# Staged attention values in 128-token groups, their copies behind the product, a conversion's sum one unit later

## The chip, the cores and the metric

The kernel runs on one core of a Trainium2 chip. Its engines work side by side, each through its own queue in program order: TensorE (PE in the profile, with its weight loads as PEld), VectorE (DVE), ScalarE (ACT) and GpSimd (POOL). SyncE (SP) issues nearly all transfers from HBM. The metric is the device time of one execution in microseconds (us), lower is better; it is the median of the runs shown.

## The reference, cut to what matters

Three layers follow one another. Only the first is touched by most of the change; the conversion belongs to the last.

```python
# 1. attention, 4 batches, 8 heads, 512 local and 32 global tokens, head width 64
s_ll = where(|i - j| <= 32, scale * q_l @ k_l.T, -1e9);  s_lg = scale * q_l @ k_g.T
out_l = softmax([s_lg, s_ll]) @ [v_g, v_l]               # a local token sees a window and the global tokens
out_g = softmax(scale * q_g @ [k_g, k_l].T) @ [v_g, v_l] # a global token sees all
# 2. soft mixture of experts: logits = x @ phi, softmax over tokens, 8 experts (w1, relu, w2), softmax over slots
# 3. relu(x @ w_in) ** 2 @ w_out
```

The weights w_in and w_out come as 8-byte floats, read here as pairs of 32-bit words. The kernel turns them into 4-byte floats itself; this is called a conversion.

## The kernel before, in words

**The attention stage** takes the local tokens in 16 blocks of 32. A unit is one block of queries with one half of the heads: `("l", s, e)` for local queries of block s, and `("g", s, e)` for the global queries against the blocks s to s+2, at every third block. There are 44 units. The loop at L703 makes one step n for each unit and a few more, and writes out a software pipeline by hand: step n takes the maximum of unit n's scores on DVE (L327, four at a time) and subtracts it on POOL (L340, called the subtraction n); takes the exponential of unit n-1 on ACT (L349); runs the scores of the next two units on PE (L317); transposes unit n-2 (L357) and copies it out of PSUM (L145 or L147); and in every second step n runs the product of weights and values of the units n-4 and n-3 (L370, `av_at`), followed on DVE by its normalization (L385 to L387). The scores of all units pass through one buffer, `s_buf`, so that the maximum of unit n+1 waits for subtraction n.

`todo[(n, pos)]` holds work for step n at position 0 (before the product), 1 (behind the product and the transposes) or 2 (behind position 1); `late[n]` holds what comes last in a step, mostly transfers. The order on each engine is this written order. SP's queue is in order too: q and k blocks (four transfers of 128 KB for 64 tokens), values, w_in pieces for conversions, and pieces of w1 and w2 for the next layer (512 KB each).

**The values.** A product reads its values from `V`, 96 rows of partitions for three blocks (block i in rows 32*(i%3)), and 32 rows for the global ones. Blocks 1 and 2 are loaded straight into `V` by one transfer (L174). The others pass through `v_next` (128 partitions), filled by transfers of 64 tokens of all batches into one half of its partitions (`load_v_next`, L179, 512 KB, seven times, two of them before the loop) and copied to `V` block by block by `place_v` (L182): batches 0 and 1 by POOL (L188), batches 2 and 3 by ACT (L186). Block s+3 takes the place of block s. It may be copied when the last product with block s's queries is done, and the next pair of products needs it. It is emitted at position 0 of the step behind that product, that is behind the subtraction of that step on POOL. Two blocks fill one transfer, and the half that they leave is loaded again at once.

**The conversions in this stage.** Eight pieces of w_in are converted by five parts: `split` and `rest`, then a step later `clamp` and `shift` (L522, L525) at position 0 and `join` at position 2. `join` makes two instructions: a bitwise one on DVE (L535), and a sum on POOL (L537), which therefore stands ahead of the next step's subtraction on POOL. Steps: `CONV` gives the unit of the first part, 4, 9, 13, 18, 22, 27, 31 and 36.

After the attention (to about 178 us of the span) come the experts and then the last layer, where further conversions run. There the parts of a conversion follow each other in the same order before and after the change.

Of the kernel before, what the change touches and what calls it, by code (L numbers as in the profile page):

```python
# [24 lines left out]
def local_global_attention__soft_moe__relu2_kernel(  # L25
# [15 lines left out]
    nc = tc.nc  # L41
# [131 lines left out]
    def load_v(i, n):  # L173
        nc.sync.dma_start(out=V[QB * i:QB * (i + n), :, :, 0:D].rearrange("p b h d -> p (b h) d"),  # L174
                          in_=v_l[:, :, QB * (i - 1):QB * (i - 1 + n), :].rearrange("b h p d -> p (b h) d"))

    def load_v_next(t):
        p = 2 * QB * (t % 2)
        nc.sync.dma_start(out=v_next[p:p + 2 * QB].rearrange("p b h d -> p (b h) d"),  # L179
                          in_=v_l[:, :, 2 * QB * t:2 * QB * (t + 1), :].rearrange("b h p d -> p (b h) d"))  # L180
# [333 lines left out]
    def convert(raw, dst, y, r, rest_on_act, add):  # L514
# [19 lines left out]
        def join():  # L534
            nc.vector.scalar_tensor_tensor(out=dst, in0=hi, scalar=-0x40000000, in1=yi, op0=ALU.bitwise_and,  # L535
                                           op1=ALU.bitwise_or)
            add.tensor_tensor(out=dst, in0=dst, in1=r, op=ALU.add)  # L537

        return [split, clamp, shift, rest, join]
# [55 lines left out]
    with tc.manual_schedule():  # L595
# [53 lines left out]
        for n in range(NC * WRES):  # L649
            split, clamp, shift, rest, join = win_convert(n)  # L650
            u = units[CONV[n]]
            for f, pos, d in ((split, 2, 0), (rest, 2, 0), (clamp, 0, CONV_AT), (shift, 0, CONV_AT), (join, 2, CONV_AT)):
                at(u, pos, f, d=d)
            if n + 1 < NC * WRES:
                after(u, win_load, n + 1, d=CONV_AT)
# [14 lines left out]
        for s in range(NJ - 2):  # L670
            n = av_at(last_of(s)) + 1
            for i, (b0, b1) in enumerate(((0, 2), (2, 4))):
                todo.setdefault((n, 0), []).insert(0, (place_v, (s + 3, b0, b1, i)))
            if s % 2 and s + 5 < NJ:
                late.setdefault(n, []).insert(0, (load_v_next, ((s + 5) // 2,)))
# [21 lines left out]
        load_v(1, 2)  # L697
        load_vg()
        load_v_next(1)
        load_v_next(2)  # L700
# [133 lines left out]
        def put_convert(q, rest_on_act, first=False):  # L834
# [7 lines left out]
            split, clamp, shift, rest, join = convert(raws[q].rearrange("p (n w) -> p n w", w=2).bitcast(I32),  # L842
# [8 lines left out]
            def last():  # L851
                join()
                room["a"].append(raws[q])
                raw_load()
# [341 lines left out]
```

## Time and profile before

| | us |
|---|---|
| three runs, median | 450.16 |
| lowest and highest of them | 447.58, 450.5 |
| the profiled execution, its own time | 451.68 |
| its span, first to last instruction | 449.9 |

Times in the rows below are microseconds from the span's start, of the one profiled execution. A row of a timeline has start, duration, engine, line, operation, what it writes and reads, and in brackets how long the engine sat idle before it and what ended that. A row of waits has who waited, for whom, the total, how often and the longest.

### The profile page before, as it was taken

What the parts mean: (1) busy time and instruction counts of PE and PEld (TensorE: products, weight loads), DVE (VectorE), ACT (ScalarE), POOL (GpSimd) and SP (SyncE); (2) the same over time, 40 slices, a digit from 0 to 9 for tenths busy, and PEclk for the clock granted to TensorE, in tenths of its full rate; (3) what the DMA queues carried; (4) which work ended last, traced back from release to release, by engine and by line L of the source; (5) the groups of instructions that cost most, each with busy time, mean ns of one, the idle gap of its engine ahead of it and who ended that gap; (6) DMA issues with size and microseconds to landing.
All of it is one profiled execution on the core that took longest, in us unless ns stands there. A gap on an engine that the chain in (4) does not pass through costs nothing.

```text
span 449.9 us, 12265 instructions
## 1 busy us (share of the span) xinstructions
PE 391.8 (87%) x4897; PEld 299.7 (67%) x4897; DVE 285.2 (63%) x911; ACT 223.2 (50%) x455; POOL 143.2 (32%) x173
## 2 busy tenths in 40 slices
PE   6847767877876876799999999999999999999996
PEld 6636555666655655435566778787787888888885
DVE  2426767666775686621089999877998544744443
ACT  1416544745865754212166657465665443444442
POOL 5215354354554553111054543233454000000000
PEclk9987979866998999999999999999999999999999
DMA  7998696989996157999993333320000410320003
GB/s 143 184 172 242 148 265 186 214 222 239 239 267 155 50 189 286 361 369 410 405 366 94 102 94 117 118 93 2 0 1 1 114 27 1 72 70 0 2 1 117
DMA packets 71145, 69.02 MB, mean 153 GB/s; under 512 B 56496, under 2 KB 56752, under 8 KB 71088
## 3 DMA queue, kind: packets, MB, share of 16 engines
q1 hardware_dynamic: 68592, 67.19, 52.3%
q10 hardware_dynamic: 2496, 1.05, 0.9%
q8 instruction: 38, 0.62, 0.6%
q14 instruction: 19, 0.16, 0.1%
HBM read 63.77 MB, written 4.46 MB: 152 GB/s over the span
## 4 chain that ended last, share of the span: by engine, by line
PE 51%; DVE 20%; DMA 9%; issue 8%; POOL 6%; ACT 3%; SPq 1%; POOLq 0%; DVEq 0%; ACTq 0%
PE ops L1129 9%; PE ops L1130 9%; PE ops L1131 8%; PE xp L370 4%; PE pp L357 3%; PE hps L905 3%; PE sp L317 3%; DVE al L1085 3%; DVE arena_a L522 3%; DMA arena_q<-in_q_l_dram 3%; POOL arena_r L340 3%; DVE arena_a L535 3%; DVE arena_b L327 2%; DMA arena_b<-in_moe_w_dram 2%; PE tp L231 2%
## 5 line engine op out<-in xcount | busy, mean ns | idle before, releaser
L1129 PE MATMUL ops<-w_hl,ah 128*128 128x512 f32 x271 | 107.1, 395 | 0.0
L1130 PE MATMUL ops<-w_hl,ah 128*128 128x512 f32 x271 | 106.6, 393 | 0.5 <-POOL w_hl L849 0.5
L1131 PE MATMUL ops<-w_hl,al 128*128 128x512 f32 x271 | 105.8, 390 | 0.0
L1078 DVE TENSOR_TENSOR arena_a<-hp,arena_a 128x384 f32<-128x384 f32 x96 | 46.8, 529 | 45.5 <-ACT arena_a L1077 45.4
L1077 ACT ACTIVATE arena_a<-hp 128x384 f32<-128x384 f32 x96 | 40.2, 471 | 62.2 <-PE hp L1074 61.9
L1084 ACT ACTIVATE ah<-arena_a 128x384 fp32r<-128x384 f32 x96 | 44.9, 504 | 27.9 <-DVE arena_a L1078 27.9
L1130 PEld LDWEIGHTS ops<-w_hl,ah 128*128 128x128 f32 x271 | 50.9, 188 | 11.5 <-POOL w_hl L849 2.7
L1131 PEld LDWEIGHTS ops<-w_hl,al 128*128 128x128 f32 x271 | 50.9, 188 | 11.1 <-DVE al L1085 0.2
L1129 PEld LDWEIGHTS ops<-w_hl,ah 128*128 128x128 f32 x271 | 50.9, 188 | 11.0 <-issue 0.8
L1085 DVE TENSOR_TENSOR al<-arena_a,ah 128x384 fp32r<-128x384 f32 x96 | 50.8, 570 | 8.9 <-ACT ah L1084 4.9
L370 PE MATMUL xp<-arena_v,arena_t 128*32 128x65 f32 x1408 | 30.6, 242 | 23.4 <-POOL arena_v L188 18.9
L340 POOL TENSOR_TENSOR arena_r<-arena_b,nm 128x512 f32<-128x512 f32 x32 | 33.7, 1052 | 51.5 <-DVE nm L327 38.7
L370 PEld LDWEIGHTS xp<-arena_v,arena_t 128*32 128x32 f32 x1408 | 25.5, 123 | 32.8 <-POOL arena_v L188 22.1
L537 POOL TENSOR_TENSOR arena_a<-arena_a 128x512 int32<-128x512 int32 x23 | 29.8, 1294 | 53.1 <-DVE arena_a L535 46.2
L317 PE MATMUL sp<-arena_b 64*32 64x128 f32 x1408 | 31.1, 300 | 6.1 <-issue 3.9
L327 DVE CUSTOM_DVE_ANT_0 arena_b<-sp,arena_r 128x128 f32<-128x128 f32 x128 | 29.4, 285 | 10.2 <-POOL arena_r L340 7.6
L147 ACT ACTIVATE arena_t<-pp 128x512 f32<-128x512 f32 x32 | 19.1, 596 | 27.2 <-PE pp L357 27.1
L357 PE MATMUL pp<-ident,arena_r 128*128 128x128 f32 x176 | 32.5, 315 | 0.0
L349 ACT ACTIVATE arena_r<-arena_r 128x512 f32<-128x512 f32 x44 | 27.6, 627 | 9.2 <-POOL arena_r L340 8.9
L317 PEld LDWEIGHTS sp<-arena_b 64*32 64x32 f32 x1408 | 22.5, 115 | 13.0 <-issue 7.5
L147 ACT ACTIVATE arena_b<-tp 128x512 f32<-128x512 f32 (+1 forms) x31 | 17.5, 579 | 27.2 <-PE tp L231 23.6
L357 PEld LDWEIGHTS pp<-ident,arena_r 128*128 128x128 f32 x176 | 21.9, 158 | 6.2 <-issue 4.1
(192 smaller groups left out, 592.3 us busy)
## 6 DMA issues: line engine op xcount, KB each, us to landing
arena_a<-in_moe_w_dram SPq DMA_DIRECT2D x34, 512.0 KB, 7.4
arena_b<-in_moe_w_dram SPq DMA_DIRECT2D x23, 512.0 KB, 7.7
arena_a<-in_moe_w_out_dram SPq DMA_DIRECT2D x16, 512.0 KB, 5.0
arena_b<-in_moe_w_in_dram SPq DMA_DIRECT2D x8, 512.0 KB, 5.5
arena_a<-in_moe_w_in_dram SPq DMA_DIRECT2D x8, 512.0 KB, 3.9
arena_k<-in_k_l_dram SPq DMA_DIRECT2D x30, 128.0 KB, 5.3
arena_q<-in_q_l_dram SPq DMA_DIRECT2D x30, 128.0 KB, 4.2
arena_b<-in_v_l_dram SPq DMA_DIRECT2D x7, 512.0 KB, 8.3
```

What stands on the lines that cost most here:

```text
L317: nc.tensor.matmul(s_t[n + e][32 * b:32 * b + 32, hp], q, keys, start=True, stop=True, tile_position=(64 * e, 32 * b))
L327: nc.vector.tensor_tensor_reduce(out=s_buf[:, j], in0=sp[:, j], in1=mk, scale=-scale, scalar=BIG, op0=ALU.add, op1=ALU.min, accum_out=nm[: ...
L340: nc.gpsimd.tensor_tensor(out=pe, in0=s_buf, in1=nm.unsqueeze(2).to_broadcast([128, 4, 128]), op=ALU.subtract)
L357: nc.tensor.transpose(pp[:, j], pe_buf[n % NPE][:, j], ident)
L370: nc.tensor.matmul(xp[32 * b:32 * b + 32, hp], pt[:, hp, 32 * b:32 * b + 32], V[:, b, 2 * hp + e], start=True, stop=True)
L1077: nc.scalar.activation(out=r[:, :N], in_=hp[:, :N], func=AF.Relu)
L1078: nc.vector.tensor_tensor(out=a[:, :N], in0=hp[:, :N], in1=r[:, :N], op=ALU.mult)
L1084: nc.scalar.activation(out=ah[:, s], in_=a, func=AF.Copy)
L1085: nc.vector.tensor_tensor(out=al[:, s], in0=a, in1=ah[:, s].bitcast(F32), op=ALU.subtract)
L1129: nc.tensor.matmul(op, ah[:, s], w_hi, start=begin, stop=False)
L1130: nc.tensor.matmul(op, ah[:, s], w_lo, start=False, stop=False)
L1131: nc.tensor.matmul(op, al[:, s], w_hi, start=False, stop=end)
```

## The change

Blocks 1 to 4, 5 to 8, 9 to 12 and 13 to 16 of the values are now loaded as groups of 128 tokens into all 128 partitions of `v_next`, by four transfers (one a batch, 256 KB each); blocks 1 and 2 pass through `v_next` too, so that two more copies run on POOL and two more on ACT, at step 2. A group is loaded again when all four of its blocks have been copied, in the steps 8, 18 and 30. A copy is emitted in the step of the last product that reads the block it replaces, at position 1 behind that product (position 2 for the first block of a group). The sum of a conversion becomes a part of its own, `plus`, emitted at position 0 of the step after `join`.

```diff
-    def load_v(i, n):
...
-    def load_v_next(t):
...
+    def load_v(g):
+        for b in range(B):
+            nc.sync.dma_start(out=v_next[:, b], in_=v_l[b, :, 128 * g:128 * (g + 1), :].rearrange("h p d -> p h d"))
...
         def join():
             nc.vector.scalar_tensor_tensor(out=dst, in0=hi, scalar=-0x40000000, in1=yi, op0=ALU.bitwise_and,
                                            op1=ALU.bitwise_or)
+
+        def plus():
             add.tensor_tensor(out=dst, in0=dst, in1=r, op=ALU.add)
...
-            for f, pos, d in ((split, 2, 0), (rest, 2, 0), (clamp, 0, CONV_AT), (shift, 0, CONV_AT), (join, 2, CONV_AT)):
+            for f, pos, d in ((split, 2, 0), (rest, 2, 0), (clamp, 0, CONV_AT), (shift, 0, CONV_AT), (join, 2, CONV_AT),
+                              (plus, 0, CONV_AT + 1)):
...
-        for s in range(NJ - 2):
-            n = av_at(last_of(s)) + 1
+        for s in range(-2, NJ - 2):
+            n = av_at(last_of(s)) if s >= 0 else 2
             for i, (b0, b1) in enumerate(((0, 2), (2, 4))):
-                todo.setdefault((n, 0), []).insert(0, (place_v, (s + 3, b0, b1, i)))
-            if s % 2 and s + 5 < NJ:
-                late.setdefault(n, []).insert(0, (load_v_next, ((s + 5) // 2,)))
+                todo.setdefault((n, 2 if s % 4 == 2 else 1), []).insert(0, (place_v, (s + 3, b0, b1, i)))
+            if s % 4 == 1 and s + 4 < NJ:
+                late.setdefault(n, []).insert(0, (load_v, ((s + 3) // 4,)))
...
-        load_v(1, 2)
+        load_v(0)
         load_vg()
-        load_v_next(1)
-        load_v_next(2)
```

On PE and DVE the order of instructions is the same before and after. It changes on POOL, ACT and SP; three places follow. In the changed kernel the line numbers are 3 to 5 smaller: the subtraction is L335, the copy on POOL L183, the sum L534, the loads of values L175.

The first place is POOL at the start of the attention, subtractions of the steps 0 to 4 (`arena_r<-arena_b`; `nm` is a unit's maximum). Before:

```order
L340 TENSOR_TENSOR arena_r_99<-arena_b_91,nm_267 128x512
L340 TENSOR_TENSOR arena_r_99<-arena_b_91,nm_285 128x512
L340 TENSOR_TENSOR arena_r_99<-arena_b_91 128x512 x2
L340 TENSOR_TENSOR arena_r_99<-arena_b_91,nm_411 128x512
L340 TENSOR_TENSOR arena_r_99<-arena_b_91,nm_473 128x512
```

After:

```order
L335 TENSOR_TENSOR arena_r_99<-arena_b_91,nm_268 128x512
L335 TENSOR_TENSOR arena_r_99<-arena_b_91,nm_286 128x512
L335 TENSOR_TENSOR arena_r_99<-arena_b_91 128x512
L183 COPY arena_v_95<-arena_b_91 32x16x64 x2
L335 TENSOR_TENSOR arena_r_99<-arena_b_91 128x512
L335 TENSOR_TENSOR arena_r_99<-arena_b_91,nm_416 128x512
```

The two copies of the blocks 1 and 2 now stand between the subtractions 2 and 3. They wait for the first load of values.

The second place is POOL a little later, from subtraction 5 on: the first sum of a conversion (`arena_a<-arena_a,arena_b`) and the copy of block 3 (`arena_v<-arena_b`). Before:

```order
L340 TENSOR_TENSOR arena_r_99<-arena_b_91,nm_473 128x512
L537 TENSOR_TENSOR arena_a_75<-arena_a_75,arena_b_91 128x512
L340 TENSOR_TENSOR arena_r_99<-arena_b_91,nm_540 128x512
L340 TENSOR_TENSOR arena_r_99<-arena_b_91,nm_599 128x512
L188 COPY arena_v_95<-arena_b_91 32x16x64
L340 TENSOR_TENSOR arena_r_99<-arena_b_91,nm_654 128x512
```

After:

```order
L335 TENSOR_TENSOR arena_r_99<-arena_b_91,nm_478 128x512
L335 TENSOR_TENSOR arena_r_99<-arena_b_91,nm_544 128x512
L534 TENSOR_TENSOR arena_a_75<-arena_a_75,arena_b_91 128x512
L183 COPY arena_v_95<-arena_b_91 32x16x64
L335 TENSOR_TENSOR arena_r_99<-arena_b_91,nm_606 128x512
L335 TENSOR_TENSOR arena_r_99<-arena_b_91,nm_659 128x512
```

The sum went from ahead of subtraction 6 to behind it, the copy from behind subtraction 7 to ahead of it.

The third place is SP late in the attention, around step 30: four transfers of k, a piece of w_in, a piece of w1, then q and values. Before:

```order
L162 DMA arena_k<-in_k_l_dram 64x8x64 x4
L512 DMA arena_b<-in_moe_w_in_dram 128x1024
L575 DMA arena_b<-in_moe_w_dram 128x1024
L162 DMA arena_q<-in_q_l_dram 64x8x64 x4
L179 DMA arena_b<-in_v_l_dram 64x32x64
```

After:

```order
L162 DMA arena_k<-in_k_l_dram 64x8x64 x4
L507 DMA arena_b<-in_moe_w_in_dram 128x1024
L572 DMA arena_b<-in_moe_w_dram 128x1024
L175 DMA arena_b<-in_v_l_dram 128x8x64 x4
L162 DMA arena_q<-in_q_l_dram 64x8x64 x4
```

A whole group of values, 1 MB instead of 512 KB, now stands ahead of the q load, where the half group stood behind it.

## Rows read from the trace of the kernel before

**Rows 1.** Busy time by stage: stretch, length, engines, PE clock, DMA share, GB/s.

```profile
60.00:108.00 48.00, 36.08 (x914) 29.06 (x918) 30.68 (x149) 26.22 (x48) 23.51 (x23) 0.79 0.89 230
...
178.00:233.00 55.00, 51.50 (x685) 27.30 (x685) 21.45 (x71) 16.63 (x40) 9.43 (x28) 1.00 1.00 391
```

**Rows 2.** Waits of DVE, 12 to 178 us.

```profile
DVE rd L385 <- PE xp L370: 10.7, 10, 1.9
DVE arena_b L327 <- POOL arena_r L340: 9.6, 13, 1.5
```

**Rows 3.** Waits of PE, 12 to 178 us.

```profile
PE xp L370 <- POOL arena_v L188: 18.9, 9, 3.5
```

**Rows 4.** Timeline of POOL, 57 to 67 us.

```profile
60.58 1.03 POOL L188 COPY arena_v<-arena_b 32x1024 f32<-32x1024 f32 x1
61.69 1.04 POOL L340 TENSOR_TENSOR arena_r<-arena_b,nm 128x512 f32<-128x512 f32 x1
```

**Rows 5.** Timeline of DVE, 60.8 to 64 us.

```profile
62.83 0.17 DVE L385 TENSOR_SCALAR rd<-xp 128x4 f32<-128x4 f32 x1 [1.92 <-PE xp L370]
```

**Rows 6.** Timeline of SP, 14.9 to 34 us: issue, duration of the issue.

```profile
14.97 0.66 SPq L174 DMA_DIRECT2D arena_v<-in_v_l_dram  x1
...
18.15 4.63 SPq L179 DMA_DIRECT2D arena_b<-in_v_l_dram  x2
...
28.92 1.79 SPq L512 DMA_DIRECT2D arena_b<-in_moe_w_in_dram  x1
```

**Rows 7.** Timeline of DVE, 33 to 38.5 us.

```profile
34.60 0.43 DVE L532 TENSOR_SCALAR arena_b<-arena_b 128x512 int32<-128x512 uint32 x1 [8.63 <-DMA arena_b<-in_moe_w_in_dram]
```

**Rows 8.** DMA view, 19 to 29 us: GB/s in 40 slices, packets of the stretch.

```profile
GB/s 230 224 178 152 143 138 121 134 142 144 168 161 172 165 162 159 154 150 141 188 164 162 162 175 177 162 157 161 163 161 153 179 147 138 145 119 138 126 182 124
DMA packets 6086, 1.58 MB, mean 158 GB/s; under 512 B 6083, under 2 KB 6083, under 8 KB 6083
```

**Rows 9.** DMA view, 129.9 to 136 us: GB/s in 40 slices.

```profile
GB/s 96 96 232 149 163 215 134 134 188 349 349 349 349 349 376 349 322 376 403 430 430 336 366 322 254 359 269 265 272 267 264 260 262 235 191 155 99 54 24 15
```

**Rows 10.** The page's part 6, q transfers: KB of one, us to landing.

```profile
arena_q<-in_q_l_dram SPq DMA_DIRECT2D x30, 128.0 KB, 4.2
```

**Rows 11.** Timeline of POOL, 73 to 77.5 us.

```profile
73.60 1.27 POOL L537 TENSOR_TENSOR arena_a<-arena_a,arena_b 128x512 int32<-128x512 int32 x1 [2.29 <-DVE arena_a L535]
74.83 1.04 POOL L340 TENSOR_TENSOR arena_r<-arena_b,nm 128x512 f32<-128x512 f32 x1
```

**Rows 12.** Timeline of DVE, 73 to 76 us.

```profile
74.01 0.28 DVE L327 CUSTOM_DVE_ANT_0 arena_b<-sp,arena_r 128x128 f32<-128x128 f32 x1
```

**Rows 13.** Timeline of PE, 129 to 146 us.

```profile
129.99 1.13 PE L370 MATMUL xp<-arena_v,arena_t 128*32 128x65 f32 x64
...
137.88 0.90 PE L231 MATMUL tp<-arena_b,arena_q 128*128 128x128 f32 x4
...
142.50 0.44 PE L317 MATMUL sp<-arena_b 64*32 64x128 f32 x10 [2.72 <-issue]
```

**Rows 14.** Timeline of SP, 127 to 142 us.

```profile
129.98 2.71 SPq L162 DMA_DIRECT2D arena_q<-in_q_l_dram  x4
```

**Rows 15.** PE groups, 61.6 to 67.6 us: busy, mean ns of one, idle before.

```profile
L357 PE MATMUL pp<-ident,arena_r 128*128 128x128 f32 x8 | 2.2, 433 | 0.0
L370 PE MATMUL xp<-arena_v,arena_t 128*32 128x65 f32 x64 | 2.0, 315 | 3.3 <-POOL arena_v L188 3.3
L317 PE MATMUL sp<-arena_b 64*32 64x128 f32 x64 | 2.0, 418 | 0.0
```

**Rows 16.** PE groups, 151.4 to 155.9 us.

```profile
L357 PE MATMUL pp<-ident,arena_r 128*128 128x128 f32 x8 | 1.3, 286 | 0.0
L317 PE MATMUL sp<-arena_b 64*32 64x128 f32 x64 | 1.2, 274 | 0.0
L370 PE MATMUL xp<-arena_v,arena_t 128*32 128x65 f32 x64 | 1.1, 221 | 1.7 <-POOL arena_v L188 1.7
```

**Rows 17.** The instructions of L525, the shift: duration ns min/median/max.

```profile
L525 DVE TENSOR_SCALAR arena_b<-arena_b x8: 426/1144/1149, 36.2 to 157.2; 128x512 int32<-128x512 int32 x8
```

More of the change, by code (lines that the diff above doesn't have):

```diff
@@ L171, in load_k @@
         load_pair(k_buf, k_l, QB * (i - 1), (1, 3) if i == 1 else ())
-    def load_v(i, n):
-        nc.sync.dma_start(out=V[QB * i:QB * (i + n), :, :, 0:D].rearrange("p b h d -> p (b h) d"),
-                          in_=v_l[:, :, QB * (i - 1):QB * (i - 1 + n), :].rearrange("b h p d -> p (b h) d"))
-    def load_v_next(t):
-        p = 2 * QB * (t % 2)
-        nc.sync.dma_start(out=v_next[p:p + 2 * QB].rearrange("p b h d -> p (b h) d"),
-                          in_=v_l[:, :, 2 * QB * t:2 * QB * (t + 1), :].rearrange("b h p d -> p (b h) d"))
+    def load_v(g):
+        for b in range(B):
+            nc.sync.dma_start(out=v_next[:, b], in_=v_l[b, :, 128 * g:128 * (g + 1), :].rearrange("h p d -> p h d"))
     def place_v(i, b0, b1, who):
@@ L536, in join @@
                                            op1=ALU.bitwise_or)
+        def plus():
             add.tensor_tensor(out=dst, in0=dst, in1=r, op=ALU.add)
-        return [split, clamp, shift, rest, join]
+        return [split, clamp, shift, rest, join, plus]
     CW = 512
@@ L649, in local_global_attention__soft_moe__relu2_kernel @@
         for n in range(NC * WRES):
-            split, clamp, shift, rest, join = win_convert(n)
+            split, clamp, shift, rest, join, plus = win_convert(n)
             u = units[CONV[n]]
-            for f, pos, d in ((split, 2, 0), (rest, 2, 0), (clamp, 0, CONV_AT), (shift, 0, CONV_AT), (join, 2, CONV_AT)):
+            for f, pos, d in ((split, 2, 0), (rest, 2, 0), (clamp, 0, CONV_AT), (shift, 0, CONV_AT), (join, 2, CONV_AT),
+                              (plus, 0, CONV_AT + 1)):
                 at(u, pos, f, d=d)
@@ L841, in put_convert @@
                 o = win2[c][:, CW * f:CW * f + CW]
-            split, clamp, shift, rest, join = convert(raws[q].rearrange("p (n w) -> p n w", w=2).bitcast(I32),
+            split, clamp, shift, rest, join, plus = convert(raws[q].rearrange("p (n w) -> p n w", w=2).bitcast(I32),
                                                       o.bitcast(I32), y[:, 0:DM], y[:, DM:].bitcast(I32),
@@ L852, in last @@
                 join()
+                plus()
                 room["a"].append(raws[q])
```

## The prediction, as it was made

> **What bounds the kernel now.** I read the busy time by stage first. From 178 to 233 us the DMA engines are full (share 1.00, 391 GB/s), so the experts' stage is set by when its transfers can start, and that is when the attention gives up its buffers [rows 1]. Behind it PE is nearly always busy in the last layer, where the change moves nothing. So a microsecond saved or lost in the attention stage goes through to the end almost whole, and only that stage has to be worked out. From 60 to 108 us no engine is full in it: PE 36.1 of 48 us at a granted clock of 0.79, DVE 30.7, POOL 23.5, while the DMA share is 0.89 [rows 1]. Such a stage is set by its chain of waits. The waits come second: PE stood still 18.9 us in nine products because the copy of a value block on POOL was not done [rows 3]; DVE waited 10.7 us for products and 9.6 us for POOL's subtraction [rows 2]. One place shows the pattern: the copy runs on POOL from 60.58 to 61.61, product and subtraction start behind it at once [rows 4, 15], and DVE, idle for 1.92 us, normalizes at 62.83 [rows 5]. Third come the transfers: at 34.60 DVE had waited 8.63 us for the first w_in piece [rows 7], issued only at 28.92 behind the values [rows 6].
>
> **The start.** Before: one value load into `V` at 14.97, then two into `v_next` [rows 6], 0.52 MB each. From 19 to 29 us, where the latter two make up most of the traffic, 256-byte packets moved at 158 GB/s [rows 8]. Each of them goes into one half of the partitions. The q load in the middle of the second stretch, with packets of the same size but spread over both halves, shows 260 to 272 GB/s [rows 9]. The new loads span all 128 partitions; I take 265 for them, the nearest row in shape, and keep 158 as the other end. DMA time removed: 2 x 0.52 MB / 158 = 6.6 us and 0.52 / 265 = 2.0 us; added: 1.05 / 265 = 4.0 us. The w_in piece lands 4.6 us earlier, near 30.0. Against it stand the two copies on POOL and the two on ACT (1.03 us each by the row of a copy [rows 4], ACT's taken alike), which now hold both engines at step 2 until the values are there: four issues of 0.66 us [rows 6] end at 17.6, the data at about 24, ACT's copies at 26, and exponential, transposition and first product follow near 27, their normalization near 29.4. That is just ahead of the new 30.0, so the wait for w_in covers the late product; if the cover is gone, it costs up to 5 us. PE's own work behind that product comes some 0.8 us later than the piece allows. I take -3.8; bounds -4.6 and +1.
>
> **The copies.** In the new order a copy waits for the product and stands ahead of the next subtraction instead of behind it, so the next product, two steps later, finds its values in place. Bounds: 0, if other waits take its place, and -18.9, PE's whole wait [rows 3]. What can reach the end is nearer to DVE's wait for products, 10.7 us [rows 2]. I take half, -5.0: DVE's next step still needs the subtraction, for which it already waits 9.6 us, and PE the copies out of PSUM. What is late next is the subtraction, then a q or k transfer. The copy's new wait for its product holds what is queued behind it on POOL, the next subtraction; but product and subtraction start together [rows 4, 15], and before the next subtraction DVE has to normalize and take four maxima, beside which a copy of 1.03 us fits.
>
> **The sum of a conversion.** Eight sums of 1.27 us stand ahead of a subtraction now. At 73.60 the sum runs until 74.87, DVE's maxima are done at 74.29, and the subtraction starts at 74.83 [rows 11, 12]: 0.5 us each at most, 8 x 0.5 = 4.0. Behind the subtraction the sum of 1.27 us stands beside DVE's four maxima, some 1.0 us (four of at most 0.28 [rows 12]), and can hold the next subtraction by 0.3 us: +2.4. I take -1.5, since DVE has other work in those steps more often than not.
>
> **Lighter transfers.** The reloads in the steps 8, 18 and 30 take 4.0 us each where their halves took 6.6. Two lie in the part where the DMA share is 0.89 [rows 1]: 0 to -5.2, I take -1.0, as most of it ends in idle DMA time. SP issues eight transfers more, 8 x 0.66 = 5.3 us; its waits for buffers to become free cover them.
>
> **New waits.** A group is loaded only when its last block is copied, and the next block is copied two steps later (in the steps 10 and 32; at 22 four steps later). At step 30 the product starts at 129.99 [rows 13]; the copies are done near 133.4, the reload's four issues end near 135.7. Only then q is issued, whose four took 2.71 us from 129.98 before [rows 14]: now until 138.4, the last landing 4.2 us [rows 10] behind its own issue at 137.7, at 141.9. PE wants q at 137.88 [rows 13]. Behind it came the scores, which in the trace stopped for 2.72 us of "issue" and ended at 142.94 [rows 13]. After: 141.9 plus transposition [rows 13] and scores [rows 16] (0.9 and 1.2 us) is 144.0, or 145 at the lower clock. I take +1.0; bounds 0 and +3.5, if that stop of 2.72 us stays behind. At step 8 the same sum leaves q just in time and ACT's copies about half a microsecond late: +0.5; bounds 0 and +3.
>
> **Sum.** -3.8 - 5.0 - 1.5 - 1.0 + 1.5 = -9.8. On the profiled execution's own 451.68 us (its span of 449.9 and 1.8 around it) that is 441.9. The median of the runs shown is 1.5 us lower, so I forecast 440.4 us, 2.2% less. From the bounds of the terms that I hold likely its own range is 436.5 to 444.5.
>
> **Rivals.** (A) PE's clock: more is gained. Behind the wait of 3.3 us that ended with the copy of 60.58 PE worked at the lower of its two levels: transposition, scores and product took 2.2, 2.0 and 2.0 us [rows 15], against 1.3, 1.2 and 1.1 us behind a wait of 1.7 us [rows 16], 2.6 us in all. If two such rounds go to the higher level, 5.2 us come on top: 435.2. For it speaks the clock of 0.79 from 60 to 108 us [rows 1]; against it, that part of PE's low clock lies behind waits for transfers. Chance 0.15.
>
> (B) No change that counts: the new loads move at 158 GB/s like the old. Then the start gives -2.8 (only 0.52 MB less), the lighter transfers nothing, step 8 costs +0.5, and at step 30 a load of 6.6 us instead of 4.0 puts q near 144.5 and the scores 3.9 us late. With k and q late, 1.5 us of the copies' gain goes: -2.8 - 3.5 - 1.5 + 0.5 + 3.9 = -3.4, some 447 us. For it speaks that all packets stay at 256 bytes; against it the rate of the q load [rows 9]. The Trainium skill (SBUF — State Buffer, "Door 1: The DMA port swizzle") says that partitions 0 to 63, or 64 to 127, reach half of the ports that a transfer over all 128 reaches; that is on the side of 265, and B would have a higher chance without it. Chance 0.2.
>
> (C) Slower: a whole group of values stands in SP's queue ahead of q, loaded late. If at both tight places (steps 8 and 30) 6.6 us of transfer at 158 GB/s find no cover and PE restarts at its lower level (0.9 us for one product, 2.0 against 1.1 [rows 15, 16]), they cost 2 x 7.5 = 15.0 us. Against -2.8 at the start, -5.0 and -1.5 that leaves +5.7: 455.9. It decides as soon as the two waits together exceed the 9.3 us of those gains. For it speaks the order of SP at step 30; against it the stop of 2.72 us that is there anyway. Chance 0.12.
>
> (D) POOL's copies hold up DVE. The shift of a conversion takes 0.43 us alone, but 1.14 us in the median [rows 17]: it runs beside a subtraction on POOL. In the steps 10, 14 and 32 a copy now follows on POOL in the step of a shift. If it gets in first, the shift waits out its 1.03 us [rows 4]: 3 x 1.03 = 3.1, and the time is 443.5. The Trainium skill (SBUF — State Buffer, "Who interferes with whom") says of DVE and GpSimd that whichever issues first holds a shared port pair for the whole instruction while the other is blocked; the two levels of the shift agree. Against D: the subtraction is first in its step, and the copy waits for its product. Chance 0.1.
>
> **How the numbers follow.** The forecast has 0.43, A 0.15, B 0.2, C 0.12, D 0.1. A measurement of this kernel tells about 1% from no change, 4.5 us: faster below 445.7, slower above 454.7. Faster: the forecast, A, D and a fifth of B, 0.43 + 0.15 + 0.1 + 0.04 = 0.72, less 0.03 for the upper edges of the forecast and D. No change: the rest of B and that, 0.16 + 0.03 = 0.19. Slower: C, 0.12. The range reaches from 433, a little under A, to 452, above B and D, and leaves out most of C.
>
> **What would show it.** Right: PE's products wait for no copy, and DVE's wait for products falls to half; DVE's first wait for w_in ends near 30; the value loads show about 265 GB/s; POOL's subtractions follow DVE's maxima without a sum between. Wrong: ACT or POOL standing at a copy for a value transfer in the steps 10 or 32, PE standing at the q transposition of step 32 for more than 4 us, or the experts' stage starting no earlier than 174 us.

## The result, and the profile after

The changed kernel takes 445.49 us (median of 20 runs, 441.55 to 450.61), the kernel before in the same comparison 450.25 us. The ratio is 0.9894 with a 95% interval of 0.9867 to 0.9921: 4.8 us faster, where 9.8 us were forecast. The direction held, and the time lies in the whole range given (433 to 452) but above the forecast's own (436.5 to 444.5); the size is a little under half of what was forecast. The profiled execution whose rows follow took 448.08 us by its own time, longer than the median.

Busy time by stage after the change, which answers to [rows 1]:

```profile
60.00:108.00 48.00, 35.40 (x956) 27.24 (x960) 34.24 (x172) 27.93 (x51) 25.05 (x26) 0.89 0.85 239
...
178.00:233.00 55.00, 52.46 (x614) 28.00 (x615) 21.49 (x67) 17.34 (x42) 11.88 (x30) 1.00 0.98 380
```

In the middle of the attention DVE and POOL do more in the same 48 us, and PE's granted clock is 0.89 instead of 0.79. The experts' stage is still full of transfers.

The waits of DVE and PE from 12 to 178 us, after the change. They answer to [rows 2, 3]:

```profile
DVE arena_b L322 <- POOL arena_r L335: 12.8, 13, 2.8
...
PE tp L226 <- DMA arena_q<-in_q_l_dram: 12.1, 4, 5.5
...
PE tp L226 <- DMA arena_k<-in_k_l_dram: 7.0, 6, 2.5
PE xp L365 <- DMA arena_v<-in_v_g_dram: 5.6, 1, 5.6
DVE rd L380 <- PE xp L365: 5.5, 5, 2.7
...
PE xp L365 <- POOL arena_v L183: 0.8, 1, 0.8
```

PE's 18.9 us of waits for POOL's copies are down to 0.8, and DVE's waits for products have halved. Two waits of PE are new: 12.1 us for q, at two places that are shown below, and 5.6 us for the first values (the row names the global values, which come last in that load).

The start, which answers to [rows 6, 7]: SP's issues of the first group and of the first w_in piece, ACT's two copies at step 2, and DVE's first use of that piece.

```profile
15.01 4.92 SPq L175 DMA_DIRECT2D arena_b<-in_v_l_dram  x4
...
25.18 0.92 SPq L507 DMA_DIRECT2D arena_b<-in_moe_w_in_dram  x1
```

```profile
25.10 2.12 ACT L181 ACTIVATE arena_v<-arena_b 32x1024 f32<-32x1024 f32 x2 [6.12 <-DMA arena_b<-in_v_l_dram]
```

```profile
30.33 0.42 DVE L527 TENSOR_SCALAR arena_b<-arena_b 128x512 int32<-128x512 uint32 x1
```

This part came as forecast: the copies wait for the values until 25.1, and DVE takes up the w_in piece at 30.33 instead of 34.60, with no wait left in front of it.

How the lead goes on can be followed on ACT. Exponential n stands once in each step, and its start in two timelines tells how far one kernel is ahead of the other. The table gives the start in the kernel before and, for the others, the difference to it, in us; the labels of the experiments are explained below.

| exponential | 5 | 10 | 20 | 31 | 32 | 43 (last) |
|---|---|---|---|---|---|---|
| before, start | 37.13 | 55.03 | 96.78 | 138.27 | 139.74 | 175.15 |
| changed kernel | -2.4 | +0.1 | -6.6 | -6.2 | +0.2 | -4.5 |
| x6, first group alone | -5.6 | -1.3 | -0.9 | -3.1 | -2.7 | -2.6 |
| x9, x6 with k ahead | -3.1 | -4.0 | -2.7 | -4.6 | -4.0 | -4.1 |
| x11, copies alone | -1.0 | +1.4 | -5.8 | -6.8 | -5.0 | -10.1 |
| y1, changed, k ahead | -3.9 | -2.3 | -11.3 | -8.8 | -2.2 | -6.9 |
| y2, changed, last group by halves | -5.3 | -3.7 | -11.6 | -10.7 | -9.5 | -12.5 |
| x10, all, halves, k ahead | -4.4 | -6.1 | -11.3 | -12.0 | -10.8 | -14.2 |

Each line of the table is one execution, so a single number of it says little: y2 and the changed kernel are issued in the same order until about step 24, and yet their leads at exponential 20 are 5.0 us apart. What repeats from one execution to the next is a fall within one step. In the changed kernel the lead goes between the exponentials 5 and 10 (by 2.5 us; the copies alone lose as much there), and all at once between 31 and 32, where 6.5 us go. Here is the second place, on POOL, SP, PE and ACT; it answers to [rows 13, 14]:

```profile
127.14 1.04 POOL L183 COPY arena_v<-arena_b 32x1024 f32<-32x1024 f32 x1 [0.31 <-PE xp L365]
```

```profile
128.21 3.84 SPq L175 DMA_DIRECT2D arena_b<-in_v_l_dram  x4
132.15 3.25 SPq L162 DMA_DIRECT2D arena_q<-in_q_l_dram  x4
```

```profile
125.88 1.13 PE L365 MATMUL xp<-arena_v,arena_t 128*32 128x65 f32 x64
...
127.52 1.16 PE L312 MATMUL sp<-arena_b 64*32 64x128 f32 x64
...
131.16 0.66 PE L352 MATMUL pp<-ident,arena_r 128*128 128x128 f32 x4
137.21 0.45 PE L226 MATMUL tp<-arena_b,arena_q 128*128 128x128 f32 x1 [5.39 <-DMA arena_q<-in_q_l_dram]
138.57 0.87 PE L226 MATMUL tp<-arena_b,arena_q 128*128 128x128 f32 x3 [0.92 <-DMA arena_q<-in_q_l_dram]
139.37 1.96 PE L312 MATMUL sp<-arena_b 64*32 64x128 f32 x64
```

```profile
136.04 1.06 ACT L181 ACTIVATE arena_v<-arena_b 32x1024 f32<-32x1024 f32 x1 [2.92 <-DMA arena_b<-in_v_l_dram]
```

The reload of the group is issued from 128.21 on, when POOL's copy is done. The four issues of q follow at 132.15. PE is ready for q at 131.8 (137.21 less 5.39) and has all of it at 138.57, and the scores behind it take 1.96 us, against the 1.16 us that such scores took at 127.52: the granted clock is 0.50 from 137 to 142 us, the lower of its two levels. ACT stands at the next copy as well. Both are signs that the prediction named as speaking against it.

These 6.3 us are only half of PE's 12.1 us for q. The other half lies between the exponentials 22 and 23, on SP and PE:

```profile
90.26 1.18 SPq L572 DMA_DIRECT2D arena_a<-in_moe_w_dram  x2
91.54 5.05 SPq L162 DMA_DIRECT2D arena_q<-in_q_l_dram  x4
```

```profile
100.76 0.47 PE L226 MATMUL tp<-arena_b,arena_q 128*128 128x128 f32 x1 [5.54 <-DMA arena_q<-in_q_l_dram]
101.52 0.90 PE L226 MATMUL tp<-arena_b,arena_q 128*128 128x128 f32 x3 [0.28 <-DMA arena_q<-in_q_l_dram]
```

This q load stands behind the reload of step 18 (84.08 to 88.00), four pieces of w1 and one of w_in. The group is not needed for the wait: x5 and x10, which load halves, stand there for 6.4 and 4.7 us. The lead falls by 1.9 us from exponential 22 to 23; no run takes this wait away by itself.

### The profile page after: what moved, and what is told of

The parts are those of the page before. It is cut to its first block, busy times and chain, and to the rows that moved or that the text cites. A ratio compares the mean times of both kernels' runs of the same rounds, so it can differ in the third digit from the quotient of the medians.

```text
span 446.3 us, 12296 instructions
## 1 busy us (share of the span) xinstructions
PE 391.1 (88%) x4897; PEld 295.9 (66%) x4897; DVE 285.1 (64%) x911; ACT 224.3 (50%) x457; POOL 144.4 (32%) x175
## 4 chain that ended last, share of the span: by engine, by line
PE 52%; DVE 17%; DMA 13%; ACT 5%; issue 5%; SPq 5%; POOL 2%; ACTq 1%; POOLq 0%; DVEq 0%
PE ops L1126 9%; PE ops L1127 9%; PE ops L1128 9%; PE sp L312 4%; DMA arena_k<-in_k_l_dram 4%; PE pp L352 3%; PE hps L902 3%; PE xp L365 3%; SPq L162 3%; DVE arena_a L517 3%; DVE arena_a L530 2%; DVE al L1082 2%; DMA arena_b<-in_moe_w_dram 2%; PE tp L226 2%; PE hp L1071 2%
## 5 line engine op out<-in xcount | busy, mean ns | idle before, releaser
L335 POOL TENSOR_TENSOR arena_r<-arena_b,nm 128x512 f32<-128x512 f32 x32 | 33.4, 1042 | 55.9 <-DVE nm L322 30.4
L534 POOL TENSOR_TENSOR arena_a<-arena_a 128x512 int32<-128x512 int32 x23 | 29.7, 1292 | 53.1 <-DVE arena_a L530 46.2
L365 PEld LDWEIGHTS xp<-arena_v,arena_t 128*32 128x32 f32 x1408 | 24.3, 116 | 24.0 <-issue 14.9
L312 PE MATMUL sp<-arena_b 64*32 64x128 f32 x1408 | 32.8, 300 | 4.9 <-ACT arena_b L147 1.8
L312 PEld LDWEIGHTS sp<-arena_b 64*32 64x32 f32 x1408 | 23.2, 115 | 12.5 <-issue 4.7
L352 PE MATMUL pp<-ident,arena_r 128*128 128x128 f32 x176 | 30.5, 300 | 0.0
L845 POOL TENSOR_TENSOR w_hl<-arena_a,w_hl 128x512 fp32r<-128x512 f32 x16 | 21.1, 1319 | 15.1 <-ACT w_hl L844 15.1
```

The lines of the kernel that those rows point to most:

```text
L312: nc.tensor.matmul(s_t[n + e][32 * b:32 * b + 32, hp], q, keys, start=True, stop=True, tile_position=(64 * e, 32 * b))
L335: nc.gpsimd.tensor_tensor(out=pe, in0=s_buf, in1=nm.unsqueeze(2).to_broadcast([128, 4, 128]), op=ALU.subtract)
L352: nc.tensor.transpose(pp[:, j], pe_buf[n % NPE][:, j], ident)
L365: nc.tensor.matmul(xp[32 * b:32 * b + 32, hp], pt[:, hp, 32 * b:32 * b + 32], V[:, b, 2 * hp + e], start=True, stop=True)
```

## Experiments

All runs are compared with the kernel before on the same chip; it measured 448.7 to 451.7 us in the comparisons, so ratios of different comparisons stand side by side only to about 0.5%. The runs x1 to x4, x5 to x8, x9 to x12, y1 to y4, and z1 with z2 are one comparison each.

| run | what differs | ratio to before, 95% | median us |
|---|---|---|---|
| x1 | copies and sum, old loads, each reload in the copy's step | 0.9925 (0.9892 to 0.9959) | 446.36 |
| x2 | group loads alone | 1.0042 (1.0008 to 1.0076) | 452.05 |
| x3 | changed kernel, q ahead of the reload | 0.9899 (0.9853 to 0.9946) | 445.66 |
| x4 | changed kernel, reloads by halves in the copy's step | 0.9940 (0.9901 to 0.9978) | 448.68 |
| x5 | changed kernel, reloads by halves one step later | 0.9816 (0.9766 to 0.9866) | 441.95 |
| x6 | first group alone | 1.0005 (0.9972 to 1.0038) | 449.49 |
| x7 | copies and sum, all transfers as before | 0.9841 (0.9799 to 0.9883) | 441.83 |
| x8 | sum alone | 0.9995 (0.9962 to 1.0029) | 448.39 |
| x9 | x6, w1 pieces behind the k load | 0.9819 (0.9776 to 0.9861) | 443.32 |
| x10 | x5, w1 pieces behind the k load | 0.9739 (0.9701 to 0.9776) | 439.51 |
| x11 | copies alone | 0.9756 (0.9716 to 0.9795) | 440.24 |
| x12 | x7, w1 pieces behind the k load | 0.9766 (0.9723 to 0.9808) | 441.37 |
| y1 | changed kernel, w1 pieces behind the k load | 0.9842 (0.9799 to 0.9884) | 442.46 |
| y2 | changed kernel, last group by halves | 0.9778 (0.9737 to 0.9818) | 439.00 |
| y3 | changed kernel, sum in its old place | 0.9879 (0.9840 to 0.9918) | 445.05 |
| y4 | x10, sum in its old place | 0.9728 (0.9684 to 0.9773) | 438.50 |
| z1 | kernel before, w1 pieces behind the k load | 0.9976 (0.9943 to 1.0008) | 448.37 |
| z2 | y1 and y2 together | 0.9774 (0.9734 to 0.9815) | 438.55 |

**The reload ahead of q.** The first theory, T1, was that copies, sum and start bring what was forecast and that the group reloads ahead of q give it back. x1 takes the copies and the sum without the group loads:

```diff
-            n = av_at(last_of(s)) + 1
+            n = av_at(last_of(s))
...
-                todo.setdefault((n, 0), []).insert(0, (place_v, (s + 3, b0, b1, i)))
+                todo.setdefault((n, 2 if s % 4 == 2 else 1), []).insert(0, (place_v, (s + 3, b0, b1, i)))
```

Expected:

> The kernel before with the copies behind the product and the sum one unit later, but with the old transfers (blocks 1 and 2 straight into V, 64 tokens into one half of v_next, reloaded in the step of the second copy). Theory T1 (the copies and the sum bring about what was forecast, and the group reloads in the queue ahead of q give much of it back): -6.5 us, ratio 0.985, which is lower than that of the changed kernel (0.989). Rival R1 (most of the measured gain is the start; copies and sum bring little, as the subtraction takes the place of the copy): -1 us, ratio 0.998. Rival R2 (a copy on POOL holds DVE's shift): as R1, with shifts of over 1.1 us in more than half of the cases.

x2 takes the group loads and leaves copies and sum where they were. Expected:

> The kernel before with the transfers of 128 tokens alone: blocks 1 and 2 pass through v_next at step 2, copies otherwise one step behind the product at position 0 as before, sum as before, a group loaded again in that later step. T1: the start gives -3.8, lighter transfers -1, and q late behind the reloads +5 or more (the reload is one step later still): 0 to +3 us, ratio 1.000 to 1.007. R1: -4 us, ratio 0.991.

x3 inserts `load_v` behind `load_q` in the list of a step. Expected:

> The changed kernel with one edit: in the steps where a group of values is loaded again, the load of q that stands in the same step (blocks 6 and 14 of the queries) is issued ahead of it. T1: PE's wait of 5.4 us for q near 137 us goes, and the time is 3 to 5 us below the changed kernel, ratio to before 0.980; the values of the next copy come 2.7 us later, which costs at most 1. If the wait only goes from q to the copies' values: ratio 0.989 as the changed kernel, with ACT and POOL standing 3 us longer at their copies in steps 10 and 32.

x4 keeps the first group and reloads with `load_v_next`, from step 2 on. Expected:

> The changed kernel with the first load of values over all 128 partitions, but each later load again of 64 tokens into one half, as soon as its two blocks are copied (six loads in the loop, from step 2 on, two steps or more of slack). T1: the start, the copies and the sum bring -3.8 - 5.0 - 1.5, nothing waits anew: 440 us, ratio 0.978. Rival: the loads at 158 GB/s in the part where the transfers fill 85% of the time delay q and k as much as the groups do: ratio 0.989 or more.

The group loads by themselves are slower, so the loads do cost (in x2 each reload stands one step later still than in the changed kernel). But x1 with no group in it misses T1's number, and its timelines of SP and PE show why:

```profile
132.66 0.62 SPq L179 DMA_DIRECT2D arena_b<-in_v_l_dram  x1
133.37 4.80 SPq L162 DMA_DIRECT2D arena_q<-in_q_l_dram  x4
```

```profile
141.01 0.45 PE L231 MATMUL tp<-arena_b,arena_q 128*128 128x128 f32 x1 [5.97 <-DMA arena_q<-in_q_l_dram]
```

The copy's earlier step had taken the reload with it, and a half of 512 KB ahead of q costs PE the same wait. In x3 q is on time, and the wait only moves to the copy, as the timelines of ACT and PE show:

```profile
140.71 1.06 ACT L181 ACTIVATE arena_v<-arena_b 32x1024 f32<-32x1024 f32 x1 [4.72 <-DMA arena_b<-in_v_l_dram]
```

```profile
141.82 0.65 PE L365 MATMUL xp<-arena_v,arena_t 128*32 128x65 f32 x28 [1.71 <-ACT arena_v L181]
```

So it is not the order of q and values that matters, as T1 had it: at this place a whole group is not loaded in time between the copy that frees it and the copy, two steps on, that needs it. x4 could not show this: its later halves stand ahead of q as in x1, and its first one stands ahead of the first w_in piece, on SP:

```profile
27.95 0.62 SPq L179 DMA_DIRECT2D arena_b<-in_v_l_dram  x1
28.61 1.37 SPq L512 DMA_DIRECT2D arena_b<-in_moe_w_in_dram  x1
```

That piece was issued at 25.18 in the changed kernel, so the start's gain was gone at once.

**The parts apart.** The second theory, T2: the reload's short time is the loss, whichever transfer goes first. x7 is x1 with each reload in its old step, one behind the copy:

```diff
-                late.setdefault(n, []).insert(0, (load_v_next, ((s + 5) // 2,)))
+                late.setdefault(n + 1, []).insert(0, (load_v_next, ((s + 5) // 2,)))
```

Expected:

> The kernel before with the copies behind the product and the sum one unit later, all transfers where they were (each reload one step behind its copy, behind q at step 31). T2: the wait of 6 us for q at step 32 that the first of these kernels showed goes, and the copies and the sum bring -6.5 us, ratio 0.9855. R3: no better than with the reload in the step of the copy, ratio 0.9925.

x5 is the changed kernel with such reloads, the first of them at step 4. Expected:

> The changed kernel with the first group of values, the copies and the sum as they are, but the later values loaded again by halves of 64 tokens in the steps of the kernel before (one step behind the copy, behind q where both meet; the half of blocks 5 and 6 at step 4, behind the first piece of w_in). Theory T2 (a group that is loaded again and needed two steps later costs a wait at steps 8 to 10 and 30 to 33, be it of q, as in the changed kernel, or of the copies, as with q issued first; nothing else was mis-sized): -3.8 - 5.0 - 1.5 = -10 us, ratio 0.977 to 0.980, and PE's waits for q and ACT's for values in the steps 8 to 10 and 30 to 33 gone. Rival R3 (the transfers as a whole bind that part: any microsecond won there turns into a wait for q or k): ratio 0.989 or more.

x6 takes only the first group. Expected:

> The kernel before with the first transfers alone changed: blocks 1 to 4 by one group over all partitions, blocks 1 and 2 copied at step 2, the half of blocks 5 and 6 loaded at step 4 behind the first piece of w_in; all later copies, loads and the sum as before. T2: -3.8 us, ratio 0.9915. R3: -1 us or nothing, as the time won at step 4 is gone by step 10.

x8 takes only the sum. Expected:

> The kernel before with the sum of a conversion alone one unit later. Forecast for this term: -1.5 us, ratio 0.9965; bounds -4.0 (0.991) and +2.4 (1.005).

x11 takes only the copies; it was set up after x5 to x8 were known. Expected:

> The kernel before with the copies behind the product alone, all transfers and the sum as before. If the sum is worth nothing in this company too, as it was alone (0.9995): ratio 0.984, as copies and sum together. If the sum brings its forecast 1.5 us only once the copies no longer stand in the way: ratio 0.9875.

T2 held for x7 and nearly for x5, and fell for the start: x6 measures no gain. The sum alone measures nothing, at most 1.7 us by its interval. The copies alone bring 11.0 us of 451.7 in x11 (0.9756). If the sum is worth nothing, x7 measures the same copies, and there they bring 7.1 us of 448.7 (0.9841). The two intervals do not meet, and nothing but the sum and the comparison differs, so the copies are known only as 7 to 11 us; by either they bring more than the 5.0 of the forecast. Waits of DVE and PE in x11, which answer to [rows 2, 3], and its busy time by stage, to [rows 1]:

```profile
DVE arena_b L327 <- POOL arena_r L340: 11.5, 16, 1.5
...
PE tp L231 <- DMA arena_k<-in_k_l_dram: 11.1, 6, 3.7
...
PE xp L370 <- DMA arena_v<-in_v_g_dram: 1.9, 1, 1.9
...
DVE rd L385 <- PE xp L370: 1.2, 3, 0.7
```

```profile
60.00:108.00 48.00, 37.52 (x1045) 29.04 (x1034) 35.55 (x175) 29.04 (x53) 27.01 (x28) 0.93 1.03 263
```

PE waits for no copy, and DVE's wait for products is all but gone, not halved. The wait for the subtraction has grown by 1.9 us only. In x7 the same two rows are 2.0 and 12.0 us. The clock from 60 to 108 us is 0.93 in x11 and 0.96 in x7.

**What takes back the start.** In the table x6 is 5.6 us ahead at exponential 5 and 1.3 at 10. SP and PE of x6 between them:

```profile
34.60 0.91 SPq L575 DMA_DIRECT2D arena_a<-in_moe_w_dram  x2
35.61 4.20 SPq L162 DMA_DIRECT2D arena_k<-in_k_l_dram  x4
```

```profile
43.71 0.45 PE L231 MATMUL tp<-arena_b,arena_k 128*128 128x128 f32 x1 [2.40 <-DMA arena_k<-in_k_l_dram]
44.83 0.87 PE L231 MATMUL tp<-arena_b,arena_k 128*128 128x128 f32 x3 [0.67 <-DMA arena_k<-in_k_l_dram]
45.49 1.06 PE L231 MATMUL tp<-arena_b,arena_q 128*128 128x128 f32 x4
46.48 1.93 PE L317 MATMUL sp<-arena_b 64*32 64x128 f32 x60
```

The k load stands behind two pieces of w1, 1 MB together; PE waits for it and goes on at the lower clock (0.50 from 43.6 to 48.5 us). Theory T3 is that this takes the start back. The edit moves the pieces from step 5 to step 7 in the table that places them:

```diff
-        0, 0, 0, 0, 1, 2, 0, 0, 1, 1, 1, 1, 0, 1, 1, 1, 0, 0, 2, 2, 1, 0, 1, 1, 0, 1, 2, 1, 0, 1, 0, 0,
+        0, 0, 0, 0, 1, 0, 0, 2, 1, 1, 1, 1, 0, 1, 1, 1, 0, 0, 2, 2, 1, 0, 1, 1, 0, 1, 2, 1, 0, 1, 0, 0,
```

x9, on x6. Expected:

> The kernel with the first group of values alone changed, and one edit more: the two pieces of w1 (512 KB each) that stand in the queue at step 5, ahead of the load of k of step 6, are issued at step 7 behind it. Theory T3 (the start does bring some 5 us until step 7, and the k load behind those pieces, whose landing PE awaits at step 8, takes most of it back): PE's wait for k near 44 us goes and 2 to 3 us come through to the end, ratio 0.994. Rival R3 (the transfers bind the whole stretch to 108 us, so the wait only moves to the next q or k): ratio 1.000 as without the edit.

x10, on x5. Expected:

> The kernel with the first group, the copies and the sum changed and the later values loaded by halves, with the two pieces of w1 of step 5 issued at step 7 behind the k load. T3: PE's wait of 5.9 us for k at step 8 goes, -3 us against the same kernel without the edit (0.9816): ratio 0.975. R3: 0.981 as without it.

x12, on x7. Expected:

> The kernel before with the copies behind the product and the sum one unit later, all value transfers as before, and the two pieces of w1 of step 5 issued at step 7 behind the k load. Without the earlier start the k load is less late there: T3 expects -1 to -2 us against the same kernel without the edit (0.9841): ratio 0.981, and the kernel with the first group on top (the run before the last) 2 us or more lower. R3: 0.984.

z1, on the kernel before. Expected:

> The kernel before with the two pieces of w1 of step 5 issued at step 7 behind the k load, and nothing else. If the k load holds up only what the earlier start has won (T3): -1 us or nothing, ratio 0.998 to 1.000, and the start is worth the difference to 0.982. If the pieces cost the kernel before as much: ratio 0.985 or less, and the start is worth 1 us or less.

In x9 the k load goes ahead of the pieces, and PE transposes it with no wait in front:

```profile
36.45 3.60 SPq L162 DMA_DIRECT2D arena_k<-in_k_l_dram  x4
40.10 1.09 SPq L575 DMA_DIRECT2D arena_a<-in_moe_w_dram  x2
```

```profile
43.91 0.81 PE L231 MATMUL tp<-arena_b,arena_k 128*128 128x128 f32 x4
44.56 0.60 PE L231 MATMUL tp<-arena_b,arena_q 128*128 128x128 f32 x4
```

The time falls to 0.9819, further than T3's 0.994, while the same edit in the kernel before (z1) brings about 1 us, 0.9976. So the start alone does bring time, once k is not late: some 7 us by the two ratios. How much is not settled, as the two traces show less: x9 is 4.1 us ahead at the last exponential, and z1, the edit without the start, is 2.0 us ahead there too. In x10 the edit brings 2.4 us on x5 by the medians and 3.5 by the ratios, near T3's 3. x12 against x7 leaves it open, 0.5 us by the medians and 3.4 by the ratios. On top of the copies the start gives little either way: 1.1 us with k late (x5 against x7, 0.9816 and 0.9841, one comparison) and 1.2 us with k on time (x10 against x12, 0.9739 and 0.9766, one comparison), where T3 had 2 or more. Where the rest of it goes there was not followed up.

**Where the changed kernel loses.** y2 keeps the groups at the start and in the steps 8 and 18, and loads blocks 13 to 16 by halves:

```diff
-            if s % 4 == 1 and s + 4 < NJ:
+            if s in (1, 5):
                 late.setdefault(n, []).insert(0, (load_v, ((s + 3) // 4,)))
+            if s in (7, 9):
+                late.setdefault(n + 1, []).insert(0, (load_v_next, ((s + 5) // 2,)))
```

Expected:

> The changed kernel with the last group of values (blocks 13 to 16, loaded at step 30) replaced by two halves of 64 tokens, each one step behind the copies that free it; the groups at the start and at the steps 8 and 18 stay. If the reload at step 30 costs what the trace shows there (the lead over the kernel before fell from 6.2 us at exponential 31 to -0.2 at 32, where the copies alone kept 5.0): 5 us less than the changed kernel, ratio 0.978. If the transfers bind that stretch anyway: 0.989.

y1. Expected:

> The changed kernel with the two pieces of w1 of step 5 issued at step 7 behind the k load. If the k load alone takes the start back in it: -6 us, as with the first group alone, ratio 0.976. If the reload of the group at step 8, whose first block is copied at step 10, holds it as well: -1 to -2 us, ratio 0.986, with ACT standing at its copy in step 10 for longer than before.

y3. Expected:

> The changed kernel with the sum of a conversion in its old place, ahead of the next subtraction. If the sum is worth nothing: ratio 0.989 as the changed kernel. If it costs 1 to 3 us beside the copies, as the two runs with and without it suggest (0.9841 and 0.9756): 0.983. If it brings its forecast 1.5 us: 0.993.

y4. Expected:

> The first group, the copies, halves for the later values and the two pieces of w1 behind the k load, with the sum in its old place: the kernel of 0.9739 without the sum's move. If the parts add up and the sum is worth nothing: 0.974. If the sum costs beside the copies: 0.970.

z2. Expected:

> The changed kernel with both edits: the two pieces of w1 of step 5 behind the k load, and the last group of values loaded by two halves, each one step behind its copies. If they add up (0.9778 and 0.9842 against 0.9894): ratio 0.973. If the k load is made up for later anyway: 0.978.

y2 settles the place. Its SP and PE, at the step that cost the changed kernel 6.5 us:

```profile
120.48 2.67 SPq L162 DMA_DIRECT2D arena_q<-in_q_l_dram  x4
124.04 0.61 SPq L179 DMA_DIRECT2D arena_b<-in_v_l_dram  x1
```

```profile
127.30 0.27 PE L231 MATMUL tp<-arena_b,arena_q 128*128 128x128 f32 x1
128.35 0.52 PE L231 MATMUL tp<-arena_b,arena_q 128*128 128x128 f32 x3 [0.78 <-DMA arena_q<-in_q_l_dram]
```

q is issued in the step of the product and PE waits 0.8 us for it instead of 6.3. The lead falls by 1.2 us between the exponentials 31 and 32, and the time is 1.16% lower than the changed kernel's, 5.2 us of 450 (6.5 by the medians). Inside one comparison the pairs give 4.6 us (y3 against y2, if the sum is worth nothing) and, with k on time, 3.1 us across two (y1 against z2), so the reload at step 30 costs 3 to 5 us. In y1, with k on time and the last group whole, 6.6 us go there again; its time, 0.9842, lies 2.3 us under the changed kernel's, nearer to the 1 to 2 us expected if the reload of step 8 holds the start as well. ACT stands in y1 at its copy in step 10, the first from that reload:

```profile
51.50 1.05 ACT L181 ACTIVATE arena_v<-arena_b 32x1024 f32<-32x1024 f32 x1 [4.33 <-DMA arena_b<-in_v_l_dram]
```

The lead there is 7.0 us at exponential 9, 2.3 at 10 and 6.2 at 11, so that reload's price is mostly made up for at once. z2 is no better than y2, so the two remedies don't add up. In y3 and y4 the sum's old place makes no difference that can be told (0.9879 beside 0.9894, 0.9728 beside 0.9739). So the 0.9% between x11 and x7 is not the sum's either. Lowest by the ratio are x10, x11, y2, y4 and z2, 0.9728 to 0.9778; they lie too close together for an order among them.

## Why the prediction was right in direction and wrong in size

Two steps made the gain half of the forecast: the reload at step 30 was taken as +1.0 us and costs 3 to 5, and the start was taken as -3.8 us and brings 0 to 1.2 as the kernel stands. A third step was wrong the other way, the copies, which hid part of it. y2, the changed kernel without the last group, gains 10.0 us and so lands on the forecast's -9.8, but only because the start's error and that of the copies cancel.

**What bounds the kernel.** Time won late in the attention goes through nearly whole: x10 is 14.2 us ahead at the last exponential and 12.8 at the end of its span, x11 10.1 and 11.8.

**The start, -3.8.** Its own steps held: the w_in piece is taken up near 30, and the late product is covered. (The piece stood behind the values and behind a k load too, which SP issued from 22.88 to 28.88 in the kernel before.) What failed is the step that charged them to the end whole ("a microsecond saved or lost in the attention stage goes through to the end almost whole"). Alone the start measures nothing (x6), because the k load behind the w1 pieces, which the prediction did not look at, is late as soon as the start is earlier. On top of the copies it brings 1.1 to 1.2 us.

**The copies, -5.0.** Right in kind, too small: 11.0 us in x11 (9.3 to 12.8 by the interval), 7.1 in x7 with the sum (5.2 to 9.0). The step that failed is "I take half": DVE's wait for products fell from 10.7 to 1.2 us in x11, and the subtraction that was to take its place added 1.9, so that 7.6 us are left of it. That is about x7's gain; what x11 has beyond it would fit rival A, the clock, but no run separates the two. The 0.93 for 0.79 from 60 to 108 us is a weak sign, as z1, with its copies as before, has 0.89 there. From 12 to 170 us the granted clock is 0.88 before, 0.86 and 0.89 in x8 and z1, and 0.94 and 0.93 in x11 and x7, so it is higher where the copies moved; how much of the gain is its own stays open.

**The sum, -1.5.** Nothing that can be told (x8, and the pairs of y3 and y4). Both bounds were too wide: x8's interval has -1.7 to +1.3.

**Lighter transfers, -1.0.** Not measured by itself; x2, with all group loads and nothing else, is 1.9 us slower than before, so what they save, with the start, is less than what their reloads cost there.

**New waits, +1.5.** The other error that made the gain smaller: the reload at step 30, taken as +1.0, costs 3.1 to 5.2 us, at its bound of 3.5 or beyond it. The transfers were reckoned well. The last q was put 11.9 us behind the product (141.9 less 129.99) and landed 12.7 behind it (138.57 less 125.88). But "PE wants q at 137.88" was read from the trace of before, 7.9 us behind the product; after the change PE was ready 5.9 us behind it, at 131.8. The 2 us between are a stop of PE in the trace of before, ahead of the last transposition of k:

```profile
136.13 0.27 PE L231 MATMUL tp<-arena_b,arena_k 128*128 128x128 f32 x1 [1.99 <-issue]
```

After the change it is not there; the trace names nothing that PE waited for, so why it went is not shown. And the stop of 2.72 us that was to cover part of the wait did not come with it, while the lower clock was named ("145") but left out of the +1.0. At step 8 the changed kernel does not show the late copy that was forecast: no copy of step 10 waits for values there; PE has stood for k before (2.49 and 0.56 us at step 8). With k on time (y1) ACT's copy is 4.33 us late, far more than the half microsecond forecast, but 3.9 of the 4.7 us that the lead loses are back at exponential 11, so the small price held. The reload of step 18 was given no wait, and PE's 5.8 us for q behind it, between the exponentials 22 and 23, was not foreseen.

**The sum of it.** Against the forecast the start missed by 3.8, the sum by 1.5 and the reloads (+5.2 for -1.0 + 1.5) by 4.7 on one side, the copies by 6.0 on the other, if x11 and y2 are taken. As measured by them: copies -11.0, start 0, sum 0, step 30 +5.2, together -5.8, where -4.8 was measured with an interval of -6.0 to -3.6. This is no check of the parts: with x7 for the copies (-7.1) the same sum is -1.9, with 3.1 for step 30 it is -7.9.

**The rivals.** (B) falls: from 85.8 to 88.4 us the reload of step 18 moved at 195 to 290 GB/s (one slice at 379), 250 in the mean; GB/s in 40 slices from 84 to 90 us:

```profile
GB/s 0 0 0 0 0 0 0 34 92 108 111 215 236 285 287 379 260 270 259 254 244 227 241 205 195 218 246 246 230 203 145 104 125 125 189 249 270 290 265 207
```

The Trainium skill (SBUF — State Buffer, "Door 1: The DMA port swizzle") has half of the ports for a transfer into half of the partitions, and 158 against some 250 GB/s agrees; that the transfers are also smaller, 256 for 512 KB, was not tried apart. Two numbers of (B) do not come out: 0.52 MB at 158 GB/s is 3.3 us, not 2.8, and q at 144.5 with 2.1 us behind it makes the scores 3.7 us late, not 3.9. (C) had the right place and mechanism at step 30; it needed twice 7.5 us and got 3 to 5 once. (D) falls: no shift takes longer than the 1.15 us of before, and four of the eight instead of six take that long (the median of 0.786 lies between the two levels):

```profile
L520 DVE TENSOR_SCALAR arena_b<-arena_b x8: 426/786/1147, 33.1 to 153.9; 128x512 int32<-128x512 int32 x8
```

## What to carry to other kernels

When a change makes a stage faster, the due times of its transfers can move with it: here q was wanted 5.9 us behind its product, not 7.9 as before. So price a late transfer against the earliest time at which its reader could be ready, with the stops in front of it taken out. A larger transfer into a buffer that is handed over whole gives up the slack that two halves had, and swapping it with its neighbour in the queue only moved the wait here. A gain early in a pipelined stage is worth what the next late transfer leaves of it (here 0 of 3.8 us), so follow the queue on to the one that is behind the largest pieces.

## What was not expected of the hardware

The issue of the phi load took 0.43 us on SP in the kernel before, behind a q load and a w1 piece, and 4.79 us in x5, where a half of the values came between:

```profile
29.65 0.62 SPq L179 DMA_DIRECT2D arena_b<-in_v_l_dram  x1
30.31 4.79 SPq L696 DMA_DIRECT2D arena_r<-in_moe_phi_dram  x1
```

It took 3.33 and 3.61 us in x6 and x9, which have that half ahead too, and 1.36 us in the changed kernel, which has not. So an issue on SP is no fixed price; what stretched it was not tried.
